# A linear-attention and token-mixing block on one core: v is not projected, h^T phi(k) is summed in four PSUM banks and multiplied by Wv afterwards; low parts of float32r splits by accumulating DMA; per-row operations on GpSimd

## The chip, the cores and the metric

The kernel runs on one core of one Trainium2 chip. Its time is the device time of one execution in microseconds; three runs before the change gave 468.1 to 470.21 us, with a median of 468.73 us. One further execution was recorded by the hardware profiler; it took 469.73 us, and its profile is the one read here. The engines are named as in the profile: PE (matrix multiplication, with PEld for its weight loads), DVE (vector), ACT (scalar and activation), POOL (GpSimd) and SP, which only issues DMAs. An engine executes its own instructions in order and waits for semaphores of others.

## The reference

The input x has S = 2048 rows of D = 448 channels; the attention has 16 heads of 28 channels.

```python
phi = lambda t: jnp.where(t > 0, t + 1, jnp.exp(t)) + 1e-6
mod = silu(c) @ w_mod                       # six vectors: sa, ca, ga, sb, cb, gb
h = layernorm(x) * (1 + ca) + sa
q, k, v = split(h @ wqkv)                   # per head
pq, pk = phi(q), phi(k)
kv = einsum("bhsd,bhse->bhde", pk, v)       # per head 28 x 28, summed over all rows
z = einsum("bhsd->bhd", pk)
o = einsum("bhqd,bhde->bhqe", pq, kv) / (einsum("bhqd,bhd->bhq", pq, z)[..., None] + 1e-6)
x = x + ga * (o @ wo)
h = layernorm(x) * (1 + cb) + sb
h = layernorm(h)
u = gelu(einsum("bsd,sf->bdf", h, w1) + b1) # token mixing: 2048 -> 1792 -> 2048
x = x + gb * transpose(einsum("bdf,fs->bds", u, w2) + b2)
```

The sums kv and z run over all rows, so no output row can be made before the last row has been projected to k and v. Since v = h Wv, the sum of phi(k)^T v over the rows is also (h^T phi(k))^T Wv.

## The kernel before, in words

The rows are worked in 16 tiles t of 128. All large products are made in float32r, with each operand split into a high part (a rounded copy, by ACT) and a low part (the operand minus the high part, by DVE: `split`, L64 and L65), as high x high + high x low + low x high. A projection of a row tile has four chunks of the 448 channels; the last, of 64, holds its high and low parts in one chunk of 128, so that a projection has 3 x 3 + 2 = 11 matmuls (`project`, L277).

The program is written in the order in which each engine shall run it (a manual schedule); tile pools add the waits. Two pools of SBUF buffers of 2 KB per partition serve nearly everything: `slots` (76 buffers) and `tok` (25). A new tile waits until the last user of the buffer that it is given has ended. PSUM has eight banks, handed out in the same way.

**Start.** The vectors ca and sa are made from c and w_mod (DVE `acc`, PE `modp`); tiles 0 and 1 get their statistics, and the weights for k and v are split.

**First loop, 16 iterations t.** PE: the k projection `kp` of tile t, the transposition `tp` of tile t+1, the v projection `vp` of tile t, and `a_kv` of tile t-1: per group of four heads one small product that adds to one PSUM bank `kvb` (113 x 448: a column of ones in front of v makes z as its first row). DVE and ACT: statistics of tile t+3 (`a_stats`, L221 to L236, whose reciprocal root is POOL's only work here), the normalisation of tile t+2 in two steps (`a_norm_a` L241, `a_norm_b` L246), the split of the transposed tile (`a_split`, hh by ACT and hl by DVE), phi(k) (`ek` by ACT L283, then DVE L284 and L285), and the copy of v (L313). In iterations 1 to 5 the weights for q are split and the other four modulation vectors are summed on DVE (`mod_acc`, L142 and L144); from iteration 7 the pieces of W1 are loaded and split (`split_to`). q is projected in this loop for tile 0 only; 15 tiles are `late`.

**Between.** Two q projections, the last kv product, then `zrow`, `kvm` (kv, masked to the heads' blocks), `zp` (z spread over the partitions) and `wp` = kv x wo, split into `wph` and `wpl`.

**Second stage, 21 iterations i.** A pipeline over row tiles: the denominators (`b_prod`, `b_sum`, `b_eps`, `b_recip`, `b_scale`) of tile i+1, the transposition `tq` of tile i, the output product `op` of tile i-1 (`b_out`, 12 matmuls), the residual and the first moments of tile i-2, the first normalisation of tile i-3, the second of tile i-4, and `step`: the product of W1 with tile i-5, into four banks `up`. The late q projections stand between these, one or two an iteration, while there are any. `b_rstd` (vw on DVE L523, rt on POOL L525) makes both reciprocal roots of an iteration. SP's queue holds all loads in order; a load waits for a free buffer.

**Rest.** The other rows of W1 in groups of up to four banks, gelu, and W2 by a scheme of seven products per block for part of the rows. The change does not touch it, apart from six pieces of W1 that are split in or just after the second stage.

Of the kernel before, what the change touches and what calls it, by code (L numbers as in the profile page):

```python
# [14 lines left out]
P = 128  # L15
# [3 lines left out]
G = 112  # L19
# [3 lines left out]
NLATE = 15  # L23
# [13 lines left out]
def block_kernel(ctx: ExitStack, tc: tile.TileContext, x, wqkv, wo, w1, b1, w2, b2, c, wmod, out):  # L37
# [34 lines left out]
    mask = cst.tile([G + 1, D], F32, name="mask")  # L72
    nc.gpsimd.memset(mask, 1.0)
    m3 = mask.rearrange("p (g h d) -> p g h d", g=4, d=DH)
    nc.gpsimd.affine_select(out=m3, in_=m3, compare_op=ALU.is_ge, fill=0.0, base=-1,
                            pattern=[[0, 4], [-DH, 4], [0, DH]], channel_multiplier=1)
    nc.gpsimd.affine_select(out=m3, in_=m3, compare_op=ALU.is_ge, fill=0.0, base=DH,
# [22 lines left out]
    def load_qkv(j):  # L100
        for ch in range(3):
            raw_w[j, ch] = slot(f"wr{j}_{ch}")
            nc.sync.dma_start(raw_w[j, ch], wqkv[ch * P:(ch + 1) * P, j * D:(j + 1) * D])
        raw_w[j, 3] = slot(f"wr{j}_3")
        for h in range(2):
            nc.sync.dma_start(raw_w[j, 3][h * 64:(h + 1) * 64, :], wqkv[384:448, j * D:(j + 1) * D])
# [6 lines left out]
    load_qkv(2)  # L113
    load_x(2)
    load_qkv(0)
# [24 lines left out]
    def mod_acc(j, n=4):  # L140
# [4 lines left out]
        macc[j] = acc  # L145

# [36 lines left out]
    def split_to(i):  # L183
        while done["split"] < min(i, len(pieces)):
# [6 lines left out]
            split(raws.pop(k), hi, lo)  # L191
# [32 lines left out]
    def a_stats(t, b6=None):  # L224
# [9 lines left out]
        nc.vector.tensor_scalar_add(ve, mv[:, 1:2], EPS)  # L234
        rs = small.tile([P, 1], F32, name=f"rs{t}", tag="rs")
        nc.gpsimd.tensor_tensor(rs, ve, mhalf[:, 0:1], op=ALU.pow)  # L236
        st[t] = (nm, rs)

    def a_norm_a(t):
        h = slot(f"h{t}", 512)  # L240
        nc.vector.scalar_tensor_tensor(h[:, :D], X[t], st[t][0], mods[1], op0=ALU.add, op1=ALU.mult)  # L241
        hs[t] = h
# [11 lines left out]
    def a_transpose(t):  # L254
        h = hs.pop(t)
# [25 lines left out]
    def phi_k(ps, name):  # L281
        dst, e = slot(f"p{name}"), slot(f"e{name}")
        nc.scalar.activation(e, ps, AF.Exp)  # L283
# [22 lines left out]
    pks, vs = {}, {}  # L306
    kvb = bank("kvb")

    def a_v(t, ps):
        v = slot(f"v{t}", 4 * (G + 1))  # L310
        v3 = v.rearrange("p (g c) -> p g c", c=G + 1)
        nc.gpsimd.memset(v3[:, :, 0:1], 1.0)
        nc.scalar.activation(v3[:, :, 1:], ps.rearrange("p (g c) -> p g c", c=G), AF.Copy)  # L313
        vs[t] = v

    def a_kv(t):
        v, pk = vs.pop(t), pks.pop(t)
        for g in range(4):
            nc.tensor.matmul(kvb[:G + 1, g * G:(g + 1) * G], v[:, g * (G + 1):(g + 1) * (G + 1)],  # L319
                             pk[:, g * G:(g + 1) * G], start=(t == 0 and g == 0), stop=(t == NT - 1),  # L320
                             skip_group_check=True)
# [29 lines left out]
    w_high(2, 0)  # L351
    w_high(2, 1)
    a_dup(1)
    w_low(2, 0)
    w_low(2, 1)
    for ch in (2, 3):
        w_high(2, ch)
        w_low(2, ch)
    wo_sb = []
    late = list(range(NT - NLATE, NT))  # L360
    MJ = (2, 4, 3, 5)
    for t in range(NT):
# [3 lines left out]
        vp = project(t, 2, "vp")  # L366
        if t == 1:
            a_transpose(t + 1)
        mp = mod_sum(MJ[t - 3]) if 3 <= t < 7 else None
        a_phi_q()  # L370
        if 0 < t < NT - 2:
            a_norm_a(t + 2)
        if t > 0 and t + 3 < NT:
            a_stats(t + 3)
        if t + 1 < NT:
            a_split(t + 1)
        if t == 0:
            m2, m3 = a_mean(2), a_mean(3)
            pks[t] = phi_k(kp, f"k{t}")
# [3 lines left out]
        if t + 2 < NT:  # L383
            a_norm_b(t + 2)
        if t > 0:
            pks[t] = phi_k(kp, f"k{t}")
        a_v(t, vp)
        if t + 2 < NT:
            a_dup(t + 2)
        if 1 <= t < 5:  # L390
            w_high(0, t - 1)
            w_low(0, t - 1)
        if t > 0:
            a_kv(t - 1)
        if t >= 5 and t - 5 not in late:
            a_q(t - 5)
        if mp is not None:
            mod_out(MJ[t - 3], mp)
        if t + 4 < NT:
            load_x(t + 4)  # L400
        if t < 4:
            load_mod(MJ[t])
        if 2 <= t < 6:
            mod_acc(MJ[t - 2])
        if t == 4:
            for g in range(4):
                w = slot(f"wo{g}", parts=G + 1)
                nc.gpsimd.memset(w[0:1, :], 0.0)
                nc.sync.dma_start(w[1:G + 1, :], wo[g * G:(g + 1) * G, :])
                wo_sb.append(w)  # L410
            b1c = cst.tile([P, NF], F32, name="b1c")
# [3 lines left out]
        if 6 <= t < 10:  # L415
            nc.vector.tensor_mul(wo_sb[t - 6], wo_sb[t - 6], mods[2][:G + 1])
        if t >= 16 - PRE:
            load_to(t + 3 - 16 + PRE)
            split_to(t + 1 - 16 + PRE)
# [3 lines left out]
    a_q(late.pop(0))  # L423
    load_to(PRE + MID + 3)
    split_to(PRE + 2)
    a_kv(NT - 1)
    zrow = cst.tile([1, D], F32, name="zrow")
    nc.scalar.activation(zrow, kvb[0:1, :D], AF.Copy)
    kvm = slot("kvm", parts=G + 1)
    nc.vector.tensor_mul(kvm, kvb[:G + 1, :D], mask)  # L430
    split_to(PRE + MID)
    a_phi_q()
    a_q(late.pop(0))
    zp = bank("zp")
    nc.tensor.matmul(zp[:, :D], ones[0:1, :], zrow, start=True, stop=True)
    zb = tslot("zb")
    nc.scalar.activation(zb, zp[:, :D], AF.Copy)
# [16 lines left out]
    def b_eps(t):  # L454
        nc.vector.tensor_scalar_add(dens[t], dens[t], 1e-6)
# [46 lines left out]
    def b_mean1(t, i):  # L502
        nms[t] = small.tile([P, 1], F32, name=f"nm{t}", tag="nm")
        nc.vector.tensor_scalar_mul(nms[t], sums.pop(t), -1.0 / D)
# [11 lines left out]
    def b_mean2(t, i):  # L516
        nm2s[t] = small.tile([P, 1], F32, name=f"ny{t}", tag="ny")
        nc.vector.tensor_scalar_mul(nm2s[t], sums.pop(t), -1.0 / D)
# [370 lines left out]
```

## Time and profile before

| What | Value |
|---|---|
| Runs, median (lowest to highest) | 468.73 us (468.1 to 470.21) |
| Profiled execution: time, span | 469.73 us, 468.0 us |
| Granted TensorE clock, mean over the span | 0.993 |
| Busy: PE, PEld, DVE, ACT, POOL | 458.6, 419.3, 360.8, 222.5, 26.2 us |
| DMA: moved, mean rate | 52.91 MB, 113 GB/s |
| DMAs issued by POOL | none |
| First loop, about | 17 to 115 us |
| Second stage, about | 127 to 235 us |

A group of instructions is named by line, engine, operation and tiles, as in `kp<-wh,hh`: kp is written from wh and hh. "Busy" counts the time in which an engine had an instruction in work; instructions of one engine overlap at their ends, so that the distance from start to start in the timeline can be shorter than the mean duration of one. The chain is the sequence of work that ended last, followed back from the last instruction; only what lies on it sets the end.

### The profile page before, as it was taken

To read this page: it belongs to the slowest core of one execution; us is meant where nothing else is said; L and a number is where in the kernel's file an instruction comes from. 1 tells how busy PE (TensorE), PEld (TensorE's weight loads), DVE (VectorE), ACT (ScalarE), POOL (GpSimd) and SP (SyncE) were. 2 spreads that over 40 slices of the span, in tenths; PEclk is the share of its full clock that TensorE was granted. 3 is DMA by queue.
4 is the path that set the end of the run, shared out by engine and by line. 5 is a ranking of instruction groups with operands and counts; after the bars stand their busy time and mean duration, and the time that the engine had idled before them with its cause. 6 is when DMAs were issued, how large, how long until landed. Compare 5 with 4: busy or idle time off the path is not lost.

```text
span 468.0 us, 7307 instructions
## 1 busy us (share of the span) xinstructions
PE 458.6 (98%) x2454; PEld 419.3 (90%) x2454; DVE 360.8 (77%) x855; ACT 222.5 (48%) x504; POOL 26.2 (6%) x62
## 2 busy tenths in 40 slices
PE   6899999999999999999999999999999999999996
PEld 4689899999799999999999999999999999999996
DVE  4789988764799877899548948609697978798992
ACT  1554334334546564666556635316565252536350
POOL 2020211100001100111100000000000000000000
PEclk8899999999999999999999999999999999999999
DMA  8999521002411101111121436215981392728312
GB/s 214 281 250 184 157 66 42 25 23 53 145 51 44 48 22 46 46 46 45 46 68 40 131 101 205 85 43 162 282 248 35 107 297 78 207 89 252 119 43 96
DMA packets 54789, 52.91 MB, mean 113 GB/s; under 512 B 8608, under 2 KB 48608, under 8 KB 54752
## 3 DMA queue, kind: packets, MB, share of 16 engines
q1 hardware_dynamic: 54752, 52.45, 39.2%
q8 instruction: 19, 0.31, 0.3%
q14 instruction: 18, 0.15, 0.1%
HBM read 45.09 MB, written 7.34 MB: 112 GB/s over the span
## 4 chain that ended last, share of the span: by engine, by line
PE 95%; DMA 1%; DVE 1%; SPq 1%; issue 0%; ACT 0%; POOL 0%; DVEq 0%
PE y L716 11%; PE up L540 10%; PE up L542 10%; PE up L541 10%; PE op L489 8%; PE vp L277 8%; PE qp L277 8%; PE kp L277 7%; PE y L717 5%; PE yp L540 4%; PE yp L542 4%; PE yp L541 4%; PE kvb L319 3%; PE tp L258 2%; PE tq L473 1%; DMA wm<-in_w_mod_dram 1%
## 5 line engine op out<-in xcount | busy, mean ns | idle before, releaser
L540 PE MATMUL up<-h2h,ph 128*128 128x448 f32 x224 | 81.8, 365 | 0.0
L541 PE MATMUL up<-h2l,ph 128*128 128x448 f32 x224 | 81.8, 365 | 0.0
L542 PE MATMUL up<-h2h,pl 128*128 128x448 f32 x224 | 81.8, 365 | 0.0
L65 DVE TENSOR_TENSOR pl<-pr,ph 128x512 fp32r<-128x512 f32 (+1 forms) x64 | 39.4, 620 | 15.5 <-ACT ph L64 12.8
L542 PEld LDWEIGHTS up<-h2h,pl 128*128 128x128 f32 x224 | 42.1, 188 | 3.3
L540 PEld LDWEIGHTS up<-h2h,ph 128*128 128x128 f32 x224 | 42.1, 188 | 3.3
L541 PEld LDWEIGHTS up<-h2l,ph 128*128 128x128 f32 x224 | 42.1, 188 | 3.3
L64 ACT ACTIVATE ph<-pr 128x512 fp32r<-128x512 f32 (+1 forms) x64 | 35.6, 567 | 12.7 <-PE up L541 6.5
L722 ACT ACTIVATE cc<-y 128x448 f32<-128x448 f32 x15 | 8.2, 545 | 56.3 <-PE y L717 47.7
L540 PE MATMUL yp<-uw,qw 128*128 128x448 f32 x84 | 31.1, 370 | 0.0
L542 PE MATMUL yp<-uw,qw 128*128 128x448 f32 x84 | 30.7, 366 | 0.0
L541 PE MATMUL yp<-uw,qw 128*128 128x448 f32 x84 | 30.7, 365 | 0.0
L477 ACT ACTIVATE pth<-tq 112x512 fp32r<-112x512 f32 x16 | 9.6, 599 | 37.8 <-PE tq L473 37.8
L637 DVE TENSOR_TENSOR u<-u,mod 128x448 f32<-128x448 f32 x14 | 8.7, 620 | 23.7 <-ACT u L636 23.7
L489 PE MATMUL op<-wph,pth 112*128 112x448 f32 x64 | 24.7, 386 | 0.0
L277 PE MATMUL kp<-wh,hh 128*128 128x448 f32 x64 | 24.6, 385 | 0.0
L277 PE MATMUL vp<-wh,hh 128*128 128x448 f32 x64 | 24.6, 384 | 0.0
L277 PE MATMUL qp<-wh,hh 128*128 128x448 f32 x64 | 24.1, 376 | 0.0
L277 PE MATMUL kp<-wh,hl 128*128 128x448 f32 x64 | 23.6, 369 | 0.1
L489 PE MATMUL op<-wpl,pth 112*128 112x448 f32 x64 | 23.5, 367 | 0.0
L277 PE MATMUL vp<-wh,hl 128*128 128x448 f32 x64 | 23.4, 366 | 0.0
L277 PE MATMUL qp<-wh,hl 128*128 128x448 f32 x64 | 23.4, 365 | 0.0
(181 smaller groups left out, 1172.3 us busy)
## 6 DMA issues: line engine op xcount, KB each, us to landing
pr<-in_B_w_dram SPq DMA_DIRECT2D x48, 256.0 KB, 2.7
a<-in_B_w_dram SPq DMA_DIRECT2D x20, 256.0 KB, 5.0
wm<-in_w_mod_dram SPq DMA_DIRECT2D x24, 196.0 KB, 6.4
a<-in_B_w_dram SPq DMA_DIRECT2D x20, 192.0 KB, 4.9
x<-in_A_x_dram SPq DMA_DIRECT2D x16, 224.0 KB, 4.4
xpark<-x SPq DMA_DIRECT2D x16, 224.0 KB, 1.9
q<-in_B_w_dram SPq DMA_DIRECT2D x28, 128.0 KB, 4.0
xb<-xpark SPq DMA_DIRECT2D x16, 224.0 KB, 4.3
```

The lines of the kernel that those rows point to most:

```text
L64: nc.scalar.activation(hi, full, AF.Copy)
L65: nc.vector.tensor_sub(lo, full, hi.bitcast(F32))
L258: nc.tensor.transpose(tps[t][:, ch * P:(ch + 1) * P], h[:, ch * P:(ch + 1) * P], ident)
L277: nc.tensor.matmul(o, a[:, s], b, start=(n == 0), stop=(n == 10))
L319: nc.tensor.matmul(kvb[:G + 1, g * G:(g + 1) * G], v[:, g * (G + 1):(g + 1) * (G + 1)], pk[:, g * G:(g + 1) * G], start=(t == 0 and g == 0 ...
L477: nc.scalar.activation(phs[t][0], tps[t][:G, :], AF.Copy)
L489: nc.tensor.matmul(opb[t][:, :D], a[:, s], b, start=(n == 0), stop=(n == 11))
L540: nc.tensor.matmul(ps[:, :D], hi[:, sl], mh, start=first, stop=False)
L541: nc.tensor.matmul(ps[:, :D], hi[:, sl], ml, start=False, stop=False)
L542: nc.tensor.matmul(ps[:, :D], lo[:, sl], mh, start=False, stop=last)
L716: nc.tensor.matmul(ps[:, :D], h[:, s], w, start=opens and r == 0, stop=False, skip_group_check=True)
L717: nc.tensor.matmul(ps[:, :HD], l[:, s], w[:, :HD], start=False, stop=closes and r == PAIRS - 1, skip_group_check=True)
```

## The change

No v is projected. In its place PE sums, for each row tile, the outer product of h (as stationary operand, not transposed) and phi(k) in four PSUM banks `cacc`, one per chunk of channels; three tiles behind kp (`KV_LAG`). For this h and phi(k) are split into high and low parts (`a_high`: xh and xl; `a_pk_parts`: pkh and pkl). After the loop the four banks are copied out (`cs`), and 16 small products with the unsplit Wv (`wr2`) give kvb. z is made apart: an accumulating DMA adds phi(k) of the tiles 1 to 14 to the buffer of tile 0, and two products with a matrix of ones give zp. The q projections of tiles 0 to 5 stand in the first loop, ten are late.

Low parts of tiles 3 to 12 and of the W1 pieces 0 to 21 are no longer subtracted by DVE: ACT writes the negated high part into the low buffer, and an accumulating DMA, issued by POOL, adds the full value. The per-row operations `ve`, `eps`, `nm`, `ny`, `vw` and `nb` move from DVE to POOL. The modulation sums are spread over eight iterations (`mod_part`). The order in the first loop changes: `a_split` is first on DVE and ACT, and `a_stats` comes after phi(k).

```diff
+Q_EARLY = (3, 4, 5)
+PIECE_DMA = range(0, 22)
+KV_LAG = 3
+DVE_LOW = (0, 1, 2, 13, 14, 15)
...
     load_qkv(1)
-    load_qkv(2)
+    load_qkv(0)
     load_x(2)
-    load_qkv(0)
     load_x(3)
...
+    def mod_part(j, k):
+        if k == 0:
+            macc[j] = slot(f"acc{j}", parts=G)
+            nc.vector.tensor_scalar_mul(macc[j], wm[j, 0], sc[:, 0:1])
+        else:
+            nc.vector.scalar_tensor_tensor(macc[j], wm[j, k], sc[:, k:k + 1], macc[j], op0=ALU.mult, op1=ALU.add)
...
-            split(raws.pop(k), hi, lo)
+            if k in PIECE_DMA:
+                full = raws.pop(k)
+                nc.scalar.activation(hi, full, AF.Copy)
+                nc.scalar.activation(lo, hi.bitcast(F32), AF.Copy, scale=-1.0)
+                nc.gpsimd.dma_start(lo, full, accum_op=ALU.add)
+            else:
+                split(raws.pop(k), hi, lo)
...
-        nm = small.tile([P, 1], F32, name=f"an{t}", tag="an")
-        nc.vector.tensor_scalar_mul(nm, mv[:, 0:1], -1.0)
         ve = small.tile([P, 1], F32, name=f"ve{t}", tag="ve")
-        nc.vector.tensor_scalar_add(ve, mv[:, 1:2], EPS)
+        nc.gpsimd.tensor_scalar_add(ve, mv[:, 1:2], EPS)
...
+    def low(t, lo, full, hi):
+        if t in DVE_LOW:
+            nc.vector.tensor_sub(lo, full, hi.bitcast(F32))
+        else:
+            nc.scalar.activation(lo, hi.bitcast(F32), AF.Copy, scale=-1.0)
+            nc.gpsimd.dma_start(lo, full, accum_op=ALU.add)
+
+    def a_high(t):
+        h = hs[t]
+        xss[t] = (slot(f"xh{t}", 512, F32R), slot(f"xl{t}", 384, F32R))
+        hi, lo = xss[t]
+        nc.scalar.activation(hi[:, :D], h[:, :D], AF.Copy)
+        nc.vector.tensor_sub(hi[:, D:], h[:, 384:D], hi[:, 384:D].bitcast(F32))
+        low(t, lo, h[:, :384], hi[:, :384])
...
+    def a_pk_parts(t):
+        pk = pkf.pop(t)
+        hi, lo = slot(f"pkh{t}", dt=F32R), slot(f"pkl{t}", dt=F32R)
+        nc.scalar.activation(hi, pk, AF.Copy)
+        low(t, lo, pk, hi)
+        if t in (0, NT - 1):
+            pksum.append(pk)
+        else:
+            nc.gpsimd.dma_start(pksum[0], pk, accum_op=ALU.add)
+        pks[t] = (hi, lo)
...
+    def a_outer(t):
+        if not cacc:
+            cacc.extend(bank(f"cacc{ch}") for ch in range(4))
+        xh, xl = xss.pop(t)
+        kh, kl = pks.pop(t)
+        for ch in range(4):
+            s = slice(ch * P, (ch + 1) * P)
+            todo = [(xh, kh), (xh, kl)] + ([(xl, kh)] if ch < 3 else [])
+            for i, (a, b) in enumerate(todo):
+                nc.tensor.matmul(cacc[ch][:, :D], a[:, s], b, start=(t == 0 and i == 0),
+                                 stop=(t == NT - 1 and i == len(todo) - 1))
...
     for t in range(NT):
         kp = project(t, 1, "kp")
         if t + 1 < NT and t != 1:
             a_transpose(t + 1)
-        vp = project(t, 2, "vp")
+        if t < KV_LAG:
+            a_q(t)
+        else:
+            a_outer(t - KV_LAG)
         if t == 1:
             a_transpose(t + 1)
+        if t in Q_EARLY:
+            a_q(t)
...
+            if t + 1 < NT:
+                a_split(t + 1)
+            if t + 2 < NT:
+                a_norm_a(t + 2)
+            a_exp(t, kp)
+            if t + 2 < NT:
+                a_norm_b(t + 2)
+            a_pk(t, kp)
+            a_phi_q()
+            a_pk_parts(t - 1)
+            if t + 3 < NT:
+                a_stats(t + 3)
+            if t >= 16 - PRE:
+                split_to(t + 1 - 16 + PRE)
+            if t + 2 < NT:
+                a_dup(t + 2)
+                a_high(t + 2)
+            if t < 4:
+                a_high(t - 1)
...
+    a_phi_q()
+    a_outer(NT - 3)
+    a_outer(NT - 2)
+    a_q(late.pop(0))
+    a_phi_q()
+    zp = bank("zp")
+    for i, pk in enumerate(pksum):
+        nc.tensor.matmul(zp[:, :D], ones, pk, start=(i == 0), stop=(i == 1))
+    a_outer(NT - 1)
...
+    a_q(late.pop(0))
+    kvb = bank("kvb")
+    for ch in range(4):
+        for g in range(4):
+            s = slice(g * G, (g + 1) * G)
+            nc.tensor.matmul(kvb[:G, s], raw_w[2, ch][:, s], csum[ch][:, s], start=(ch == 0 and g == 0),
+                             stop=(ch == 3), skip_group_check=True)
...
-        nc.vector.tensor_scalar_add(dens[t], dens[t], 1e-6)
+        nc.gpsimd.tensor_scalar_add(dens[t], dens[t], 1e-6)
...
-        nc.vector.tensor_scalar(ve[:, lo:hi], vss.pop(i)[:, lo:hi], 1.0 / D, EPS, op0=ALU.mult, op1=ALU.add)
+        nc.gpsimd.tensor_scalar(ve[:, lo:hi], vss.pop(i)[:, lo:hi], 1.0 / D, EPS, op0=ALU.mult, op1=ALU.add)
...
-        nc.vector.tensor_mul(nb, nm2s.pop(t), rs)
+        nc.gpsimd.tensor_mul(nb, nm2s.pop(t), rs)
```

The two `tensor_scalar_mul` of `b_mean1` (nm) and `b_mean2` (ny) change from `nc.vector` to `nc.gpsimd` in the same way. In the first loop the modulation products `modp` stand in iterations 4, 6, 8 and 10 and their sums in iterations 2 to 9; `wo` is multiplied by ga in iterations 7 to 10.

More of the change, by code (lines that the diff above doesn't have):

```diff
@@ L279, in project, with a_exp, phi_k @@
         return o
-    def phi_k(ps, name):
-        dst, e = slot(f"p{name}"), slot(f"e{name}")
-        nc.scalar.activation(e, ps, AF.Exp)
+    eks = {}
+    def a_exp(t, ps):
+        eks[t] = slot(f"ek{t}")
+        nc.scalar.activation(eks[t], ps, AF.Exp)
+    def phi_k(t, ps, new):
+        dst, e = new(f"pk{t}"), eks.pop(t)
         nc.vector.tensor_scalar(e, e, 1.0, 1e-6, op0=ALU.min, op1=ALU.add)
@@ L350, in block_kernel @@
     a_norm_b(1)
-    w_high(2, 0)
-    w_high(2, 1)
+    w_high(0, 0)
+    w_high(0, 1)
     a_dup(1)
-    w_low(2, 0)
-    w_low(2, 1)
+    w_low(0, 0)
+    w_low(0, 1)
     for ch in (2, 3):
-        w_high(2, ch)
-        w_low(2, ch)
+        w_high(0, ch)
+        w_low(0, ch)
     wo_sb = []
-    late = list(range(NT - NLATE, NT))
+    late = [t for t in range(KV_LAG, NT) if t not in Q_EARLY]
     MJ = (2, 4, 3, 5)
@@ L547, in step @@
             acc3(ps, hi, lo, slice(i * P, (i + 1) * P), mh, ml, first, last)
+    a_q(late.pop(0))
     for fn in (b_prod, b_sum, b_eps, b_recip, b_scale):
@@ L558, in block_kernel @@
         Wpl.append(lo)
-    a_q(late.pop(0))
     accs, early = None, []
```

125 lines of the change are left out of this document (52 added, 73 removed).

## The prediction

> **What bounds the kernel now.** I read first the page's busy shares and its chain (section 4), then busy time by stretch of 10 us, then the chain in order of time, and last single rows of the timeline for prices.
>
> ```profile
> PE 458.6 (98%) x2454; PEld 419.3 (90%) x2454; DVE 360.8 (77%) x855; ACT 222.5 (48%) x504; POOL 26.2 (6%) x62
> ...
> PE 95%; DMA 1%; DVE 1%; SPq 1%; issue 0%; ACT 0%; POOL 0%; DVEq 0%
> ```
>
> The matrix engine is busy for 98% of the span and is 95% of the chain: what counts is PE work taken out, minus new PE waits. Stretches of the attention part (columns PE, PEld, DVE, ACT, POOL, then clock, DMA share, GB/s):
>
> ```profile
> 20.00:30.00 10.00, 8.97 (x51) 8.09 (x51) 8.34 (x20) 6.43 (x18) 2.17 (x6) 1.00 1.08 253
> 40.00:50.00 10.00, 10.00 (x57) 8.71 (x56) 9.69 (x23) 3.98 (x10) 2.58 (x7) 1.00 0.88 189
> 70.00:80.00 10.00, 10.00 (x58) 9.24 (x58) 8.50 (x20) 3.74 (x8) 1.20 (x4) 1.00 0.18 51
> 200.00:210.00 10.00, 10.00 (x55) 9.22 (x54) 9.82 (x32) 6.45 (x15) 1.38 (x2) 1.00 0.19 54
> ```
>
> After 30 us PE never rests, though DVE is nearly full at 40:50 and 200:210; ACT is half idle, POOL almost idle, and the DMA share falls to 0.2 after 60 us. One iteration of the loop over row tiles in the chain (start, us, what):
>
> ```profile
> 75.71 2.25 PE kp L277 x11
> 77.96 0.44 PE tp L258 x4
> 78.40 2.23 PE vp L277 x11
> 80.63 0.79 PE kvb L319 x8
> ...
> 120.65 0.94 PE zp L435 x2
> 121.59 3.19 PE wp L553 x8
> ```
>
> So one iteration is 2.25 + 0.44 + 2.24 + 0.79 = 5.72 us of PE. The last rows show what POOL and DVE do to each other, and the landing times of DMAs:
>
> ```profile
> 19.16 0.69 DVE L241 SCALAR_TENSOR_TENSOR h<-x,an,mod 128x448 f32<-128x448 f32 x1
> 19.26 0.99 POOL L236 TENSOR_TENSOR rs<-ve,mhalf 128x1 f32<-128x1 f32 x1 [13.25 <-DVE ve L234]
> 34.05 0.55 POOL L236 TENSOR_TENSOR rs<-ve,mhalf 128x1 f32<-128x1 f32 x1 [4.38 <-DVE ve L234]
> 48.55 1.94 POOL L408 MEMSET wo<- 1x448 f32 x4
> 48.98 0.69 DVE L284 TENSOR_SCALAR ek<-ek 128x448 f32<-128x448 f32 x1
> 56.34 0.38 DVE L284 TENSOR_SCALAR ek<-ek 128x448 f32<-128x448 f32 x1
> ...
> wm<-in_w_mod_dram SPq DMA_DIRECT2D x24, 196.0 KB, 6.4
> ...
> xpark<-x SPq DMA_DIRECT2D x16, 224.0 KB, 1.9
> ```
>
> **The change, part by part.** *PE.* Removed: 16 v projections (16 x 2.24 = 35.8), 16 groups of kv products (16 x 0.79 = 12.6), the row product zp (0.94): 49.4. Added: 16 outer products of 11 matmuls of the same shape as a projection (35.8), 16 small products with Wv (0.79 / 4 each = 3.2), two full products for z (0.75 each by the modp rows of the chain = 1.5): 40.5. The q projections and wp only change place. Net **-8.9 us**. One kv group gains nothing: the first ran at 28.9 to 29.6, while PE waited for hh and hl of the next tile until 30.27, and it will now simply wait: **+0.8**.
>
> *Start.* ve of tile 1 goes to POOL ahead of rs, on the path to h(1), for which PE waits 1.4 us (tp at 21.03). A POOL row of one column costs 0.55, the DVE row it replaces 0.14: **+0.4** (0 if the wait has other slack, 0.99 by the slow rs row). The qkv weights arrive four to six DMAs earlier; DVE and ACT rows, not landings, fill 16 to 28 us, so I count no gain.
>
> *DVE in the loop,* start to start from the timeline at 82 to 88 us: norm_a 0.59, bn 0.66, aggr 0.21, hl 0.61, norm_b 0.59, ek 0.42, pk 0.54, a new 64-column subtraction 0.13 (estimate, by the one-column rows): 3.75 us; nm, ve and the piece's pl (0.61) are gone. Iterations 1 and 2 add phi_q 0.54, low parts on DVE 1.0 to 1.15, and at 2 two mod parts 1.05: 5.4 and 6.5 against PE's new 4.93 (kp, tp, and q or outer). That is a lag of 2.1 us; hl(t+1) has 2.24 - 0.60 (hh) - 0.69 (hl) = 0.95, plus some 0.3 for the two matmuls that need only hh. So PE waits **+0.8** (0 to 2.1). At iterations 7 to 9 (mod parts and wo: 5.6, 5.4, 5.6 against 4.93, 5.68, 4.93) the lag peaks at 1.05, within the slack.
>
> *ACT in the loop:* hh 0.49, ek 0.43, dup 0.17, four hi and negated copies of x and pk (0.47 to 0.57), two per piece (0.62 and 0.55): 4.4 us, below 4.93. The v copy (0.54) is gone. Costed at nothing; PE's 4.93 hides it.
>
> *POOL and its DMAs.* POOL now issues 56 accumulating DMAs of 192 to 256 KB: 10 for xl, 10 for pkl, 14 that sum pk, 22 for W1 pieces. Iterations 7 to 10 have four each, 11 to 13 three. No row shows such a DMA. Its issue cost c lies between 0.10 (POOL's cheapest row, a memset of one column) and 1.9 (xpark's whole landing, as if POOL were held so long); I take the middle, 1.0. With ve and rs (1.2 together) POOL needs 5.2 us against 5.3 of PE (mean of iterations 7 to 10, two with a modp product): just enough. Behind a late DMA on POOL stand the next ve and rs; DVE's norm_b waits for them, then tp and kp. They have about an iteration's slack, 5 us. Landing: 1.9 (xpark) to 6.4 (wm, at DMA share 1.08); I take 3, since the share here is 0.2. xl is needed three iterations later, pkl about one and a half: hidden. The sum of pk is serial, each DMA waiting for the last to land, 14 in 14 iterations of 4.9 us or more: hidden at 3. Its tail is not free: the last iterations reuse buffers that DMAs of the iteration before still read (ek of tile 14 waits for the sum of pk 12 and for pkl 12), and zp waits for the last sum. **+1.0** (0 to 6.5).
>
> [...]
>
> *Between loop and second stage.* The four copies of the outer sums (ACT and DVE, two each at about 0.55) hide behind the q projection after them (2.24), kvm (0.62) behind the q projection before wp. Without these covers 1.1 and 0.6 would be added. Of the 10 late q projections 7 remain for the second stage (12 of 15 before), so its PE period falls to 5.3 us from the sixth iteration on.
>
> *Second stage.* eps, nm, ny, vw and nb leave DVE (about 0.5 us an iteration with their gaps; DVE is 98% full at 200:210) for POOL at 0.55 to 0.69 each. The loop that carries itself is norm1_b 0.68, eps 0.55 (queued ahead), ny 0.55, sqb 0.86, vw 0.55, rt 0.69: 3.9 us against 5.3. Every third iteration a W1 DMA stands ahead of vw on POOL and waits for ACT's two copies: about 2 more, 5.9 once in three. **+0.7** (0 to 8).
>
> *Sum:* -8.9 + 0.8 + 0.4 + 0.8 + 1.0 + 0.7 = **-5.2 us**. The profiled execution took 469.73 us with a span of 468.0; its span should become 462.8 and its time 464.5. The median of the runs is 1.0 below that execution: 468.73 - 5.2 = **463.5 us**.
>
> **The rivals.** *1, slower: POOL's issue.* If c is large, POOL is the bound of iterations 7 to 13. Its lag is 4 x (4c + 1.2 - 5.3) + 3 x (3c + 1.2 - 4.93) = 25c - 27.6. Less 5 us of slack it eats the gain of 5.2 at c = 1.5, where this decides. At c = 1.9 the lag is 19.9, so +14.9 - 5.2: 478.4 us. For it: nothing else in the kernel issues from POOL, and POOL's smallest arithmetic already takes 0.55. Against: SP's queue issues every load of before and is 1% of the chain. Chance 0.15.
>
> *2, slower: the DMA engines.* An accumulation reads its target too. At 7 to 10 it is 896 KB of accumulation and 480 KB of loads an iteration: 260 GB/s in 5.3 us, under the 297 that the fullest slice of the page moved. Counted twice, accumulation makes 2272 KB, 7.65 us at 297: +2.35 x 4; at 11 to 13 about 1.9 MB, 6.4 us: +1.5 x 3. That is 13.9, less 5 slack: +8.9 - 5.2, 472.4 us. It decides from a weight of about 1.6. For it: transfers land in 6.4 us where the share is 1.08. Against: reads from SBUF need no HBM. Chance 0.16.
>
> *3, about even: POOL and DVE block each other in the second stage.* The rs row took 0.99 beside a two-input DVE instruction and 0.55 otherwise; ek took 0.69 beside POOL memsets and 0.38 otherwise. With 0.99 for each of eps, ny, vw and rt the carried loop is 5.5, with the DMA about 6.2 on average: 0.9 x 11 iterations, less one iteration's slack: +4.6, or about 468 us. Against: the DVE rows beside rs at 26 us keep 0.67 to 0.69. Chance 0.13. [...]
>
> **How the numbers follow.** 0.5% (2.3 us) is about what a measurement of this kernel can tell from no change. My forecast has 0.56; its own range is 458.5 (all waits nil: -8.9, and 1.3 for unseen gains) to 466.4. Faster 0.56 (the forecast), within 0.5% 0.13 (rival 3), slower 0.31 (rivals 1 and 2). The range for eight in ten, 458.5 to 477, leaves out about half of rival 1 and a little below.
>
> **What would show it.** PE's busy time near 450 with no vp rows, 176 outer matmuls, and about 3 us more of PE waits, before 40 us and around 100 to 115. DMA share 0.6 to 0.9 at 60 to 100 us. POOL's gaps between rs rows no longer than PE's iteration (4.9 to 5.7): longer ones, with norm_b waiting for POOL, mean rival 1; landings of POOL's DMAs above 5 us, rival 2; norm1_b or recip waiting for POOL at 160 to 230 us, rival 3. A wait of PE at zp or wp of over 1 us would make the tail wrong.

## The result, and the profile after

The changed kernel takes 471.83 us (median; 470.11 to 472.94), the kernel before 468.46 us beside it. The ratio is 1.0054 with a 95% interval of 1.0031 to 1.0077: slower by 0.5%. The forecast was 463.5 us.

The profiled execution took 470.11 us with a span of 468.4 us (before: 469.73 and 468.0). The page, busy time by engine, and the chain:

```profile
PE 451.6 (96%) x2360; PEld 410.7 (88%) x2360; DVE 344.5 (74%) x750; ACT 252.5 (54%) x559; POOL 107.7 (23%) x193
...
PE 84%; ACT 3%; DVE 3%; DMA 3%; POOL 3%; issue 2%; SPq 0%; POOLq 0%; ACTq 0%; DVEq 0%
```

PE's work fell by 7.0 us (458.6 before), but its idle time grew from 9.4 to 16.8 us. The chain, 95% PE before, now has ACT, DVE, DMA and POOL in it. Where this is, the stretches tell (PE, PEld, DVE, ACT, POOL, then clock, DMA share, GB/s):

```profile
70.00:80.00 10.00, 10.00 (x53) 8.92 (x52) 9.29 (x19) 8.72 (x19) 7.32 (x9) 1.00 1.08 228
80.00:90.00 10.00, 9.54 (x48) 8.02 (x47) 7.66 (x17) 7.47 (x16) 6.70 (x10) 1.00 1.02 184
90.00:100.00 10.00, 8.34 (x42) 6.65 (x41) 6.87 (x16) 5.82 (x12) 6.88 (x9) 1.00 1.06 199
100.00:110.00 10.00, 6.40 (x27) 5.32 (x26) 4.53 (x9) 3.94 (x8) 5.60 (x7) 0.79 0.71 127
110.00:120.00 10.00, 10.00 (x45) 9.15 (x45) 3.10 (x6) 4.70 (x9) 3.48 (x4) 0.87 0.87 167
...
180.00:190.00 10.00, 9.57 (x52) 8.53 (x51) 9.80 (x25) 7.14 (x16) 5.45 (x14) 1.00 0.17 54
```

From 40 to 80 us PE is full, as forecast. From 80 to 107 us (four waits, in iterations 11 to 14 of the first loop) it stands idle for 5.7 us. In the last of these waits the granted clock falls; its mean is 0.79 and 0.87 in the stretches from 100 and from 110 us. In the chain in order of time, the eleven outer matmuls at 107.65 us last 4.11 us where others last 2.23, and the kp after them 2.65: another 2.3 us. The DMA share is 1.00 or more in every stretch from 40 to 100 us; before the change it was 0.40 on average at 40 to 80. What PE waited for (us in total, times, longest):

```profile
PE tp L274 <- ACT h L266: 3.6, 1, 3.6
PE tp L274 <- DVE h L262: 3.6, 4, 1.5
```

Of the second row 1.5 us belong to the start. All the rest, 5.7 us, is one place: the transposes of the next tile (in the longest wait only the last of the four, which also reads a copy of 64 columns of h). The chain in order of time shows what is late ahead of them:

```profile
82.99 0.87 POOL pk L359
83.86 0.28 POOL ve L249
...
84.22 0.58 POOL rs L251
84.80 0.02 issue
84.83 0.70 DVE h L262
...
98.83 0.89 POOL pkl L336
99.72 0.61 issue
100.33 4.73 DMA pk<-pk
...
105.22 0.04 ACT pkl L335
...
105.70 0.62 ACT ph L204
...
106.89 0.25 ACT h L266
107.13 0.04 issue
107.18 0.47 PE tp L274
```

Two mechanisms. At 83 us the statistics of a tile (ve, rs on POOL) stand behind the DMA that sums pk, and h waits for rs. At 100 us a sum of pk takes 4.73 us to land; ACT waits for it, since its next tile (pkl) was given a buffer that this sum still reads; ACT's rows follow in program order (pkl at 105.22, ph at 105.70, pl at 106.35, h at 106.89 us), so the small copy `h` (64 columns), which the last transpose needs, stands behind it. ACT's own waits for sums, at 40 to 120 us (us in total, times, longest), show it:

```profile
ACT ek L301 <- DMA pk<-pk: 5.3, 2, 3.4
ACT pkl L335 <- DMA pk<-pk: 3.1, 1, 3.1
```

What held POOL ahead of its sum DMAs in the same stretch:

```profile
POOL pk L359 <- DMA pk<-pk: 7.9, 5, 3.4
POOL pk L359 <- issue: 4.7, 6, 1.7
```

The first row is the serial sum, each DMA waiting for the landing of the last. The second has no releaser in the profile. At 60 to 110 us, where the loss is made, the second has all of its 4.7 us and the first only 1.3.

One caution on the two profiles. Executions differ in the clock of the first matmuls: at 10 to 15 us it was 0.50 in the profile of before and 1.00 in that of after, and the transposes of tile 1 began at 21.03 and 19.20 us. That is not the change: with the same code up to there, other runs below have 0.50 to 0.55 and 20.2 to 22.0 us, or 0.83 to 1.00 and 18.9 to 20.1 us. After's profiled execution is 1.7 us faster than the median of its runs, for which this start is the likely reason (the other executions were not profiled), and the loss that the prediction did not see is nearer to 8.3 us (471.8 against 463.5) than to the 5.6 of the profiles (468.4 against 462.8).

### The profile page after: what moved, and what is told of

Its sections match the earlier page's. It is cut to its first block, busy times and chain, and to the rows that moved or that the text cites. A ratio compares the mean times of both kernels' runs of the same rounds, so it can differ in the third digit from the quotient of the medians.

```text
span 468.4 us, 7285 instructions
## 1 busy us (share of the span) xinstructions
PE 451.6 (96%) x2360; PEld 410.7 (88%) x2360; DVE 344.5 (74%) x750; ACT 252.5 (54%) x559; POOL 107.7 (23%) x193
## 3 DMA queue, kind: packets, MB, share of 16 engines
q1 hardware_dynamic: 54752, 52.45, 37.6%
q0 software_dynamic: 8064, 13.24, 16.8%
HBM read 45.09 MB, written 7.34 MB: 112 GB/s over the span
## 4 chain that ended last, share of the span: by engine, by line
PE 84%; ACT 3%; DVE 3%; DMA 3%; POOL 3%; issue 2%; SPq 0%; POOLq 0%; ACTq 0%; DVEq 0%
PE y L796 11%; PE up L621 9%; PE up L622 9%; PE up L620 9%; PE qp L293 7%; PE op L569 7%; PE cacc L374 6%; PE y L797 5%; PE kp L293 4%; PE yp L620 4%; PE yp L622 4%; PE yp L621 4%; PE tq L553 1%; DMA wr<-in_A_wqkv_dram 1%; DMA pk<-pk 1%
## 5 line engine op out<-in xcount | busy, mean ns | idle before, releaser
L69 DVE TENSOR_TENSOR pl<-pr,ph 128x512 fp32r<-128x512 f32 (+1 forms) x42 | 24.6, 585 | 9.3 <-ACT ph L68 8.2
L206 POOL DMA_DIRECT2D pl<-pr x22 | 21.0, 956 | 36.9 <-ACT pl L205 35.1
L68 ACT ACTIVATE ph<-pr 128x512 fp32r<-128x512 f32 (+1 forms) x42 | 22.3, 539 | 10.8 <-PE up L621 5.0
L374 PE MATMUL cacc<-pkh,xh 128*128 128x448 f32 x64 | 25.6, 401 | 0.0
L374 PE MATMUL cacc<-pkl,xh 128*128 128x448 f32 x64 | 24.3, 380 | 0.0
```

What stands on the lines that cost most here:

```text
L68: nc.scalar.activation(hi, full, AF.Copy)
L69: nc.vector.tensor_sub(lo, full, hi.bitcast(F32))
L206: nc.gpsimd.dma_start(lo, full, accum_op=ALU.add)
L374: nc.tensor.matmul(cacc[ch][:, :D], a[:, s], b, start=(t == 0 and i == 0), stop=(t == NT - 1 and i == len(todo) - 1))
```

## The experiments

Each is an edit of the changed kernel. "Effect" is the difference of its ratio from 1.0054, times 469 us. The kernels of e6, e7, e13 and e14 leave out part of the computation and serve for their time alone.

The expectations speak of five theories of what makes PE wait: 1, POOL's queue (statistics behind DMAs that wait); 2, the DMA engines are full; 3, ACT's added copies; 4, POOL waits for room for the descriptors of its DMAs (the kernel sets it, `dynamic_dma_scratch_size`); 5, buffers that DMAs hold until they land.

| Run | Edit | us (before beside it) | Ratio, 95% interval | Effect, us |
|---|---|---|---|---|
| e1 | no W1 piece by DMA | 464.24 (469.53) | 0.9874 (0.9845 to 0.9904) | -8.4 |
| e2 | statistics ahead of the pk DMAs | 471.68 (469.53) | 1.0064 (1.0040 to 1.0087) | +0.5 |
| e3 | pk summed by DVE | 464.74 (469.53) | 0.9904 (0.9869 to 0.9940) | -7.0 |
| e4 | 4096 bytes for descriptors | 468.07 (469.53) | 0.9973 (0.9956 to 0.9990) | -3.8 |
| e5 | 78 buffers | 470.74 (469.33) | 1.0041 (1.0016 to 1.0067) | -0.6 |
| e6 | piece DMAs of 64 columns | 468.45 (469.33) | 0.9978 (0.9960 to 0.9996) | -3.6 |
| e7 | sum DMAs of 64 columns | 467.13 (469.33) | 0.9967 (0.9949 to 0.9984) | -4.1 |
| e8 | 3 pieces by DMA, 4096 bytes | 463.78 (469.33) | 0.9878 (0.9847 to 0.9910) | -8.3 |
| e9 | ACT's small copy first | 475.16 (469.42) | 1.0124 (1.0104 to 1.0145) | +3.3 |
| e10 | e9 and e4 | 473.96 (469.42) | 1.0104 (1.0081 to 1.0127) | +2.3 |
| e11 | e8, per-row work on DVE | 465.19 (469.42) | 0.9901 (0.9876 to 0.9927) | -7.2 |
| e12 | e8, last three sums by DVE | 462.54 (469.42) | 0.9857 (0.9835 to 0.9880) | -9.2 |
| e13 | no piece DMA, copies stay | 461.61 (468.77) | 0.9849 (0.9824 to 0.9875) | -9.6 |
| e14 | piece DMA copies, one ACT copy | 464.84 (468.77) | 0.9911 (0.9878 to 0.9943) | -6.7 |
| e15 | two running sums | 471.39 (468.77) | 1.0058 (1.0033 to 1.0083) | +0.2 |
| e16 | pieces 3 to 8 by DVE | 465.41 (468.77) | 0.9934 (0.9914 to 0.9955) | -5.6 |
| e17 | e15 and 3072 bytes | 466.62 (468.73) | 0.9958 (0.9936 to 0.9980) | -4.5 |
| e18 | 3072 bytes, buffers freed | 466.86 (468.73) | 0.9956 (0.9930 to 0.9981) | -4.6 |

**First four: whose DMAs, and what they hold.**

```diff
-PIECE_DMA = range(0, 22)
+PIECE_DMA = ()
```

> The 22 W1 pieces go back to the split of before (ACT copies the high part, DVE subtracts), so POOL issues 34 accumulating DMAs instead of 56 and ACT loses 22 copies of about 0.55 us; DVE gets 22 subtractions of about 0.59 back. After stands at 471.8 us, with 16.8 us of PE idle against 9.4 before. Theory 1 (order on POOL: rs stands behind accumulating DMAs that wait for the landing of the one before, and then PE's transposes wait): one DMA in four leaves the queue, the sum of pk stays serial, so about half of the 5.7 us of PE idle at 80 to 107 us goes: 467 to 469. Theory 2 (the DMA engines are full): 22 of 56 accumulations go, the share of 1.0 at 70 to 100 us falls to about 0.7 and landings to about 3 us, the idle goes altogether: 462 to 465. Theory 3 (ACT's added copies make the buffers late): the same as theory 2 with landings unchanged at 4.2 to 4.5 us.

Effect -8.4 us: all of what the forecast had missed. The loop loses nothing after 90 us; what it loses at 79 to 86 us is DVE's, which now has the pieces and modulation sums together:

```profile
80.00:90.00 10.00, 9.05 (x45) 7.78 (x46) 9.62 (x20) 5.64 (x14) 6.13 (x8) 1.00 0.92 184
90.00:100.00 10.00, 10.00 (x54) 9.14 (x53) 9.65 (x21) 7.16 (x16) 7.79 (x10) 1.00 0.89 169
100.00:110.00 10.00, 10.00 (x52) 9.19 (x52) 8.16 (x17) 5.43 (x11) 3.88 (x5) 1.00 0.63 127
```

The landings of the other DMAs did not fall to 3 us (pk 4.6, pkl 4.4 at 60 to 110 us), against theory 2 as I had put it; the DMA share only from 1.06 to 0.89.

```diff
+            if t + 3 < NT:
+                a_stats(t + 3)
             a_pk_parts(t - 1)
-            if t + 3 < NT:
-                a_stats(t + 3)
```

> Only the order on POOL (and DVE's statistics) in the loop is changed: the statistics of tile t+3 come ahead of the low part of pk and of the sum of pk of tile t-1. All DMAs stay. Theory 1 (rs behind the pk DMAs): tp no longer waits for h (1.5 us in all, 80 to 100 us) and perhaps the wait for ACT at 106 us (3.6) shrinks: 467 to 470. Theory 2 (DMA engines full): landings stay at 4.2 to 4.5 us and so does the time, 471 to 473. Theory 3 (ACT's copies): unchanged, 471 to 473.

No gain. The waits of tp for DVE's h at 80 to 100 us went, and PE waited for the landings of pkl instead (3.3 us in four waits), beside ACT's copy (2.6): moved back, these DMAs landed too late. The order alone, theory 1 in its plain form, is not the cause.

```diff
-            nc.gpsimd.dma_start(pksum[0], pk, accum_op=ALU.add)
+            nc.vector.tensor_add(pksum[0], pksum[0], pk)
```

> The sum of pk over tiles is made by 14 DVE additions (about 0.55 us each) in place of 14 accumulating DMAs; the other 42 DMAs stay. DVE has 3.75 us of work in a PE iteration of 4.9, so the additions should hide except at iterations 2, and 7 to 9 (0 to 1 us). Theory 1: the serial chain of waits leaves POOL, rs is on time, ACT's wait of 3.4 us for a buffer that a sum still reads goes, and the clock does not fall after it: 5 to 8 us less, 464 to 467. Theory 2: a quarter of the accumulated bytes goes, so 1 to 3 us less, 469 to 471. Theory 3: unchanged or slightly slower, 471 to 473.

Effect -7.0, as theory 1 had it. But e1 and e3 take away different DMAs and each gives nearly everything, so neither set is the cause by itself; the sum of both is too much.

```diff
-dynamic_dma_scratch_size=1024
+dynamic_dma_scratch_size=4096
```

> Only the memory kept for descriptors of DMAs that POOL issues is four times as large (4096 bytes in place of 1024). Theory 4 (the waits without a visible releaser ahead of the sum DMAs, 0.4 to 1.7 us each, are POOL waiting for room for descriptors): those waits go, and 3 to 6 us of the idle with them: 466 to 469. Theories 1 to 3: unchanged within 1 us, 471 to 473.

Effect -3.8. The waits without a releaser went (4.7 us in after, 0.2 here) with this memory as the only edit, so they were for room for descriptors. POOL's waiting did not go (40 to 120 us, rows as above):

```profile
POOL pk L359 <- DMA pk<-pk: 14.5, 8, 3.5
...
POOL pk L359 <- issue: 0.2, 1, 0.2
```

The wait at 100 to 107 us stayed (3.3 us, with a granted clock of 0.87 at 100 to 110 us), and the landings of pkl grew from 4.4 to 5.7 us.

**Next four: buffers and bytes.**

```diff
-NSLOT, NTOK = 76, 25
+NSLOT, NTOK = 78, 25
```

> Only the number of buffers in the large pool is changed, from 76 to 78. In the profile of after, ACT waited 3.1 us at 102 us for a buffer that a sum DMA still read, and PE's transposes 3.6 us for that. Theory 5 (the buffers: with a landing of 4.5 us instead of 3 a buffer comes free one instruction too late): two more buffers let that one wait shrink, 2 to 4 us less, 468 to 470. Theory 1 (POOL's queue: four DMAs of 0.9 us, each sum behind the landing of the last, do not fit in PE's 4.93 us, so the lag grows whatever the number of buffers): under 1 us less, 471 to 472.5.

Effect -0.6, within the intervals. ACT's wait only moved to another instruction (pl for a sum, 3.1 us). Two buffers are too few to judge the theory by.

```diff
-                nc.gpsimd.dma_start(lo, full, accum_op=ALU.add)
+                nc.gpsimd.dma_start(lo[:, :64], full[:, :64], accum_op=ALU.add)
```

> The 22 DMAs of the W1 pieces stay in POOL's queue, with ACT's two copies and with their buffers, but each moves 64 of its 512 columns, 32 KB instead of 256; the other columns of the low part are left wrong, so this kernel leaves out part of the computation. Theory 2 (bytes: the DMA engines are full): most of the 7.6 us that taking these DMAs away gained comes here too, 464 to 466. Theory 1 (their places in POOL's queue and their issue time) and theory 3 (ACT's copies): 469 to 472. Landings of pl shorter than 2.5 us and the share lower at 60 to 110 us would show that the bytes are gone.

Effect -3.6 of the 8.4 that the pieces cost: bytes are a part, not all. Those of 32 KB land in 3.4 us, and in the same stretch (60 to 110 us) those of 192 KB in 3.5 (256 KB in after: 4.3), so most of these landings is not the DMA's own bytes:

```profile
xl<-h POOLq DMA_DIRECT2D x6, 192.0 KB, 3.5
pl<-pr POOLq DMA_DIRECT2D x7, 32.0 KB, 3.4
```

PE lost nothing at 80 to 100 us, but the wait at 101 to 105 us stayed (4.0 us, clock 0.50 for 6.8 us).

```diff
-            nc.gpsimd.dma_start(pksum[0], pk, accum_op=ALU.add)
+            nc.gpsimd.dma_start(pksum[0][:, :64], pk[:, :64], accum_op=ALU.add)
```

> The 14 DMAs that sum pk stay, each still waiting for the landing of the one before, but each moves 64 of its 448 columns (the other columns of z are left out of the sum). Theory 1 in the form that the landing time of the serial chain holds POOL: the sums land in about 2 to 2.5 us, no DMA waits for the last, and the time is that of the kernel with the sum on DVE without its added DVE work, 463 to 466. In the form that it is the number of DMAs, at 0.9 us of issue each: 469 to 472. Theory 2: a quarter of the accumulated bytes less, 468 to 470.

Effect -4.1. The sums land in 3.6 us, and at 60 to 110 us POOL no longer waits for that, but 4.6 us without a releaser; PE's wait at 104 to 107 us shrank from 3.6 to 2.7. Between the two forms of theory 1.

```diff
-PIECE_DMA = range(0, 22)
+PIECE_DMA = range(0, 3)
-dynamic_dma_scratch_size=1024
+dynamic_dma_scratch_size=4096
```

> The low parts of the first three W1 pieces only (the iterations in which DVE also makes modulation parts) stay with POOL's DMAs, the other 19 go to DVE, and the memory for descriptors is 4096 bytes. The kernel with no piece on POOL took 464.24 and lost 1.2 us of PE at 80 to 86 us to DVE work (hl 0.76, the modulation sum 0.47); after 86 us its loop lost nothing. If POOL has room for one more DMA in iterations 7 to 9, these 1.2 us come back: 462 to 463.5. If three pieces are enough to make POOL late again, 464 to 467.

463.78, between the two expected ranges and not told apart from e1. Its profile loses 0.2 us at 80 to 90 (e1: 0.95) and 0.5 at 110 to 120 us.

**Order again, the second stage, and a better version.**

```diff
             a_phi_q()
+            if t + 2 < NT:
+                a_dup(t + 2)
             a_pk_parts(t - 1)
...
             if t + 2 < NT:
-                a_dup(t + 2)
                 a_high(t + 2)
```

> All DMAs and buffers of after stay; only ACT's small copy of 64 columns of h (0.26 us), for which PE's transposes of tile 15 waited 3.6 us, is issued ahead of the copies of pk and of the W1 piece in its iteration, and no longer behind the copy that waits for a sum's landing. Theory 5a (one late landing holds ACT, which works in order; what costs is who stands behind it): the transposes start on time, hh of tile 15 is then the next behind the wait, needed about 2.7 us later, so 1.5 to 2 of the 3.6 us go, and the fall of the clock after it becomes smaller: 2 to 4 us less, 468 to 470. Theory 1 (POOL's queue has grown too long, everything behind it is late by the same amount): the lag stays and shows at the next wait, under 1 us less, 471 to 472.5.

A miss of both theories: 3.3 us slower. The wait that it aimed at is gone, but ACT now waits for DVE's h ahead of its copies of pk, the pieces and xh (at 40 to 120 us; in after 5.2 us in six waits):

```profile
ACT h L266 <- DVE h L262: 16.6, 8, 2.6
```

In the chain at 58 to 90 us ACT's copies (pkh, pkl, ph, xh) and DVE's work (64 columns of xh, modulation sums, hl, both halves of h) stand one after the other, and from one xh to the next it takes 5.4 to 7.1 us. Of theory 5a the run says nothing.

The next run is this one with 4096 bytes for descriptors, as in e4.

> The order of the run before with 4096 bytes for descriptors. The larger memory took 3.7 us off after and left one wait of 3.3 us, the one that the order is to shorten. If the two are separate causes, their gains add: 464.5 to 467. If they are the same lag seen twice, the time is that of the larger memory alone: 467.5 to 469.

Slower by the same loop: the same kinds of waits as in e9, and the larger memory gives 1 us. Nothing of the question is answered.

```diff
-        nc.gpsimd.tensor_scalar_add(dens[t], dens[t], 1e-6)
+        nc.vector.tensor_scalar_add(dens[t], dens[t], 1e-6)
...
```

and in the same way nm, ny, vw and nb.

> Built on the kernel with three pieces on POOL (463.78): the per-row operations of the second stage (eps, nm, ny, vw, nb; the change moved them to POOL) go back to DVE. Rival 3 of the prediction (POOL's per-row chain is what costs in the second stage): 0.5 to 1 us less, 462.8 to 463.3. If they relieve DVE, which shows 9.3 to 10.0 of 10 us at 170 to 190 us there: DVE gets about 0.5 us an iteration more, the stage gets DVE bound for some of its 16 iterations, 1 to 4 us more, 465 to 468.

465.19 against e8's 463.78, with intervals that overlap: not told apart. Rival 3's gain is not there; the profile hints at the other side (PE 9.55 and 9.74 of 10 us at 160 to 180 us with 33 DVE instructions in the second).

```diff
-        else:
+        elif t < 12:
             nc.gpsimd.dma_start(pksum[0], pk, accum_op=ALU.add)
+        else:
+            nc.vector.tensor_add(pksum[0], pksum[0], pk)
```

on top of e8.

> Built on the same kernel: the last three sums that were DMAs (tiles 12 to 14) are DVE additions, since ACT there still waits 3.5 us for a sum's landing and PE 0.5 us for what follows (outer products at 110 to 120 us). If the landings at the loop's tail still cost: 0.5 to 1 us less, 462.8 to 463.3. If DVE's 0.55 us each come in the way at the tail, nothing or a loss: 463.8 to 465.

462.54 us, ratio 0.9857 (0.9835 to 0.9880): the lowest median of the complete kernels here, faster than before by 1.4% and than after by 2.0%; from e1 and e8 its interval does not tell it apart. The page and two stretches:

```profile
PE 450.0 (98%) x2360; PEld 409.2 (89%) x2360; DVE 357.3 (78%) x772; ACT 241.5 (52%) x540; POOL 93.6 (20%) x171
```

```profile
90.00:100.00 10.00, 9.73 (x52) 8.37 (x51) 9.09 (x20) 6.68 (x15) 6.33 (x10) 1.00 0.85 169
100.00:110.00 10.00, 10.00 (x52) 9.05 (x52) 8.63 (x18) 4.89 (x10) 1.93 (x2) 1.00 0.47 100
```

**Last six: which of the three things that e1 takes away at once.**

```diff
                 nc.scalar.activation(lo, hi.bitcast(F32), AF.Copy, scale=-1.0)
-                nc.gpsimd.dma_start(lo, full, accum_op=ALU.add)
```

> The 22 piece DMAs are left out, and with them part of the computation (the low parts of these W1 pieces stay the negated high parts); ACT's two copies of each piece, the sums of pk and all other DMAs stay. Theory 1 and 5 (queue places and landings): as good as moving the pieces to DVE, 463 to 465. Theory 3 (ACT's copies are what makes the iteration long): most of the loss stays, 469 to 472.

Effect -9.6: theory 3 falls. ACT's copies, all still there (252.0 us busy), cost nothing without the DMAs.

```diff
-                nc.scalar.activation(lo, hi.bitcast(F32), AF.Copy, scale=-1.0)
-                nc.gpsimd.dma_start(lo, full, accum_op=ALU.add)
+                nc.gpsimd.dma_start(lo.bitcast(F32), full)
```

> The 22 piece DMAs stay in POOL's queue, but copy the piece instead of adding it to a negated high part, so ACT's second copy of each piece (0.62 us) is left out, and with it part of the computation (the low part becomes the whole piece). Theory 3 (ACT's copies): 464 to 467. Theory 1 and 5: the queue and the landings are as before and only fewer bytes are read, 468 to 471.

Effect -6.7, in theory 3's range, but e13 says that it is not for theory 3's reason. The same 22 DMAs of 256 KB are cheaper without accumulation. POOL's queue, first of after and then of e14 (packets, MB, share of 16 engines):

```profile
q0 software_dynamic: 8064, 13.24, 16.8%
```

```profile
q0 software_dynamic: 6656, 13.24, 13.2%
```

56 accumulating DMAs made 8064 packets, 144 each; with 34 of them, 22 plain ones made 80 each. The waits for room fell from 4.7 to 0.6 us. So the run changes more than the copy, and cannot stand for theory 3.

```diff
-        if t in (0, NT - 1):
+        if t in (0, 1, NT - 1):
...
-            nc.gpsimd.dma_start(pksum[0], pk, accum_op=ALU.add)
+            nc.gpsimd.dma_start(pksum[t % 2], pk, accum_op=ALU.add)
```

and 77 buffers.

> Two running sums of pk (even and odd tiles) in place of one, so a sum DMA waits for the landing of the last but one, about 10 us earlier, and never really waits; one product more for z (0.75 us of PE) and one buffer more (77), since the second sum holds one through the loop. Everything else stays. Theory 1 in the form that the serial wait on POOL is the cause: the gain of the sum on DVE, less 0.75: 465 to 467. If it is the landing that holds the buffers for ACT (theory 5), or the number of DMAs: 470 to 473.

Effect +0.2: the serial wait by itself is not the cause. It is gone, and POOL waits longer for room instead (4.7 us in after):

```profile
POOL pk L359 <- issue: 8.3, 8, 2.2
```

```diff
-PIECE_DMA = range(0, 22)
+PIECE_DMA = (0, 1, 2) + tuple(range(9, 22))
```

> Only pieces 3 to 8, those of the loop's iterations 10 to 15, go back to DVE; pieces 0 to 2 and 9 to 21 (after the loop) stay with POOL's DMAs. If the loss is made at 80 to 115 us alone: 463.5 to 465. If the DMAs behind the loop (9 to 21, POOL beside the per-row operations of the second stage, where after loses 0.6 us of PE at 170 to 190 us) cost as well: 465 to 467.

Effect -5.6: the pieces of iterations 10 to 15 make most of the loss, the other 16 the rest to e1 (2.8 us). Of that, PE waits 1.4 us more than in e1 for DVE's h in the first loop, which e8 (4096 bytes, the same three early pieces) does not, and loses 0.5 us at 170 to 180 us (e1: 0.1).

The next run is e15 with 3072 bytes for descriptors.

> Two running sums of pk and 3072 bytes for descriptors together (77 buffers, of which the second sum holds one): neither of the two waits that POOL had ahead of a sum DMA should be left. The two sums alone gave 471.39, the memory alone (4096 bytes) 468.07. If POOL's waits are the cause: 465 to 467. If they are not, and ACT's waits for buffers that DMAs still read are: 468 to 470, with PE's wait of about 3 us for ACT at 100 to 107 us still there.

Effect -4.5, in the first range. POOL has neither wait left, but now its DMAs are issued sooner and land later: at 60 to 110 us the sums in 6.6 us (4.4 in after), xl in 6.6 (4.5), with a share of 1.12 at 80 to 100 us. ACT still waits for buffers (pkh for a sum 2.7), PE 1.1 and 2.3 us for it.

```diff
-NSLOT, NTOK = 76, 25
+NSLOT, NTOK = 77, 25
...
-            load_to(t + 4 - 16 + PRE)
+            load_to(t + 2 - 16 + PRE)
```

and 3072 bytes.

> One running sum as in after, 3072 bytes for descriptors, and about three buffers more for the loop: 77 in place of 76, and each W1 piece is loaded two iterations later (one ahead of its use in place of three). POOL still waits for the landing of the last sum. If ACT's waits for buffers are what is left with the larger memory: the wait of 3 us at 100 to 107 us goes, 464 to 466. If POOL's serial wait is what is left: 467 to 469.

Effect -4.6, between the ranges. The wait of 3 us at 100 to 107 us is gone, which fits a buffer that a DMA still read (the edit also moves the loads of the pieces, so the run does not test the buffers alone). Small ones took its place (PE for h 0.4, pkl's landing 0.9, hh 0.7, pkl 0.7), with landings of 4.9 (pl) to 6.2 us (pkl).

**What follows.** The 56 accumulating DMAs are too much for iterations 7 to 13, and three limits stand behind each other: room for descriptors (POOL waits 4.7 us for it in after), buffers held until a landing (ACT waits 3.1 us for one in the longest wait of PE), and the DMA engines themselves (a share of 1.04 at 60 to 100 us). Lift one and the next holds: e4 trades POOL's waits for room (4.7 to 0.2 us) against its waits for landings (7.9 to 14.5), e15 the reverse (4.7 to 8.3 for room, 7.9 to none for landings), e17 and e18 lift two and the landings grow to 4.9 to 6.6 us. These gains don't add (e4 -3.8, e18 -4.6), while fewer DMAs give all of it (e1 -8.4, e13 -9.6). How much of the loss is each limit's own is therefore not a number that these runs give, and where only landings grew, that full engines are the reason is read from the share and not tested alone.

## Why the prediction was wrong

- **PE, net -8.9: right within 0.7.** PE is busy for 450.0 to 450.4 us in e1, e12 and e13 against 458.6, that is -8.2 to -8.6. In after it is 451.6, with the slow clock at 107 to 113 us, which costs 2.3 us.
- **First kv group +0.8 and DVE lag +0.8: somewhat smaller.** PE waits 0.7 us for hh and 0.3 for hl before 40 us: 1.0 against 1.6.
- **Start +0.4: smaller.** The wait of tp for h is 1.5 us against 1.4.
- **ACT at nothing: right** by e13, as long as no buffer is late.
- **POOL's issue, c = 1.0: about right.** Its DMA rows last 0.89 to 0.98 us in the mean. Rival 1 asked for 1.5. But the step that followed, "POOL needs 5.2 us against 5.3 of PE: just enough", counted POOL's work and none of its own waits: 12.6 us ahead of 14 sums, 6.0 of them at 60 to 110 us. From one rs to the next went 7.26, 7.19, 5.62, 6.49 and 5.36 us at 70 to 102 us, which is what I had named as the sign of rival 1. The sign alone does not decide, though: e12 has 7.35 and 6.57 too, but then 4.41, and PE loses 0.4 us.
- **Landing 3, and DMA waits at the tail +1.0 (0 to 6.5): the term that failed.** The landing was taken at the DMA share of the kernel before (0.2); the share that the new DMAs make is 1.04 at 60 to 100 us (0.6 to 0.9 had been named), and the landings are 4.3 to 4.5 us. The mechanism was named in that step (buffers that DMAs still read), its place and price were not. The very wait that it named, ek of tile 14 for the sum of pk 12, is there (3.4 us) and PE loses nothing by it. What costs is one iteration earlier: pkl of tile 12, and behind it in ACT's order the copy of h. With POOL's late statistics PE waits 5.7 us at 80 to 107 us, and the clock that falls in the longest wait costs 2.3: 8.0 us in place of 1.0, beyond the upper bound, which left the clock out.
- **The sum, term by term, in the two profiles.** PE's idle time grew by 7.4 us where 3.7 were forecast: 1.1 before 40 us (2.0 forecast), 5.7 at 80 to 107 us (1.0), 0.6 in the second stage (0.7). PE's busy time fell by 7.0 and not 8.9, mainly for the 2.3 of the slow clock. Together that is the 5.6 us of the profiles. The other 2.7 of the 8.3 are differences between executions: the forecast's 1.0 from profile to median, and the 1.7 by which after's profile is faster than its median.
- **Rival 2: refused too lightly, and yet not what happened.** In the profile of after POOL's queue takes 16.8% of 468.4 us for 13.24 MB, 5.94 us per MB, SP's 37.6% for 52.45 MB, 3.36: a weight of 1.77, where the rival was to decide from 1.6. That reads from SBUF need no HBM holds here (45.09 MB read from HBM and 7.34 written in the profiles of before and of after alike, with POOL's 13.24 MB in after alone), but it was no argument, as it is the engines that are full (the share of 1.04). But 472.4 us is its sum for a weight of 2. With 1.77 the same sum has a lag of 9.5, less 5 of slack, which takes back 4.5 of the 5.2: about 468 us, so 1.6 was too low a bound (about 1.8 eats the gain). That 472.4 is near the result is luck; bytes are one of the three limits (e6: -3.6 for seven eighths of the pieces' bytes). Its KB, too, are of 1024 bytes: 2272 of them take 7.8 us at 297 GB/s, not 7.65.
- **Second stage +0.7: right in size.** PE loses 0.13 and 0.43 us at 170 to 190 us. The chain there goes as the term said: ACT's copies of a piece, POOL's DMA, then vw, rt and nb. The sign of rival 3 did appear, norm1_b (DVE's y) waiting for POOL's rt, 7.7 us in five waits at 160 to 230 us (1.2 in e1, without piece DMAs), but these waits cost PE no more than that 0.6 us.

## What to carry to other kernels

The DMAs that do arithmetic for a busy engine were not free here (8.4 us for the 22 of the pieces, e1), where the DMA engines (a share of 1.04 at 60 to 100 us), POOL's queue (12.6 us of waits ahead of its sums) and the buffers (9.6 us of ACT's waits for sums at 40 to 120 us) were all near their limit. Price such a DMA per iteration on each of the three, with its bytes weighted, its landing taken at the share that it makes itself, and each buffer held until that landing. When the saving is on PE, look for the in-order queue in which a waiting instruction stands ahead of the one that PE needs. Moving work by DMA in the iterations that have room (here three pieces and eleven sums) and leaving it on DVE elsewhere kept the saving (e12, 462.54 us).

## What the runs showed of the hardware

- An accumulating DMA from SBUF to SBUF made 144 packets in the mean for its 128 rows (of 192 to 256 KB in all), a plain one of 256 KB 80; per MB it took 5.94 us of all 16 engines (after), against 2.84 for the plain copies (e14: 13.2% of 460.4 us is 60.8, less 7.47 MB at 5.94, over 5.77 MB).
- Its landing hardly depended on its own size: at 60 to 110 us, in the same trace, 3.4 us for 32 KB and 3.5 to 4.1 for 192 to 224 KB (e6), 3.6 for 32 KB and 3.7 to 4.1 for 192 to 256 KB (e7). It was longer where nothing held POOL from issuing: 5.9 to 6.6 us in e17, 4.3 to 4.5 in after.
- The granted clock fell to 0.50 at short gaps of PE, for 3.4 us (e2, e4, e5, e7, e15) or twice that, 6.8 us (after, e6). These lengths are estimates from the clock of the stretches, at 0.50 for as long as it is low: in e2 0.64 and 0.51 in the two of 2 us from 102 us; in after 0.93, 0.50 three times and 0.87 in the five of 2 us from 104 us; in e4 0.87 and 0.96 in the two of 10 us from 100 us. The gap alone does not decide: it fell at gaps of 4.0 (e6), 3.6 (after), 3.4 (e15), 3.3 (e4), 3.1 (e5) and 2.7 us (e7), and in e2 at one of 1.5 us; it did not after 2.3 us (e17), nor after 2.1 us in e2 itself.
